# A 768-token windowed attention with a routed expert layer: second weights ordered behind row gathers, and one copy moved from ScalarE to VectorE

## The chip, the cores and the metric

The kernel runs on one core of one Trainium2 chip. The metric is the device time of one execution in microseconds; less is better. The engines are called as in the profile: PE (matrix products), PEld (its weight loads), DVE (VectorE), ACT (ScalarE), POOL (GpSimd) and SP (which issues most transfers here). An engine works through its own instructions in order, and waits on semaphores for the others and for transfers.

## The reference

Everything is float32. An attention with a local window and a few global keys makes x; each row of x then goes to one of eight experts, chosen by the largest cosine logit, and the expert's two products are scaled by the gate.

```python
batch, n_heads, seq, head_dim = (4, 8, 768, 64)
...
a = np.exp(scores)
a = a / (np.sum(a, axis=-1, keepdims=True) + 1e-09)
return np.matmul(a, v).astype(np.float32)
...
logits = xn @ en.T / tau
expert_idx = np.argmax(logits, axis=1)
...
for e in range(E):
    mask = expert_idx == e
    h = np.maximum(x[mask] @ w1[e], 0.0)
    out[mask] = gate_w[mask, None] * (h @ w2[e])
```

x has 3072 rows of 512; w1 of an expert is 512 x 1024 and w2 is 1024 x 512, 2 MB each.

## The kernel before, in words

The first 184 us compute the attention and the routing, and write x and a list of rows per expert to HBM. The first 256 rows of expert 0 are handled at the end of that part. Then a loop over the eight experts begins (L1880 on); an expert's rows that remain are padded to one of several widths.

In the loop, expert e is multiplied while the rows and weights of the next one ("coming") are fetched:

- **Rows.** POOL gathers rows of x by index. For experts 0 and 1 it gathers whole rows of 2 KB, 128 at a time (`gather_tiles`, L1056). From expert 2 on it gathers quarters: 16 gathers per expert, each of 128 quarter rows of 512 bytes (`gather_quarters`, L1082). While expert e runs, POOL issues the last eight quarters of expert e+1, then the scatters of results that are pending, then the first eight quarters of expert e+2, and then a drain. For expert 2 the first four come ahead and the other twelve in one go. Every two gathers after the first four, a tiny POOL copy (`landed`, L1081) waits until an earlier pair has landed; it holds the pace.
- **Weights.** SP loads w1 in four transfers of 512 KB (L169) and w2 in one of 2 MB (L170), both in `load_weights`. Two sets of buffers are used in turn. The first w1 transfer waits for a product of the expert before (`n.out_again`; for expert 2, for a scatter). The w2 transfer has no wait but that its buffer is free, which is when the expert two places earlier has done its last product. For experts 0 and 1 the weights come in 32 pieces of 128 KB each (`load_weights_part`, L182): 16 of w1, then 16 of w2. Those that the attention part has not issued are left in `n.weights` (L909): here three pieces of w1 and sixteen of w2, all of expert 1. The first of these waits for expert 0's first two row gathers.
- **Products.** The width of an expert selects an arm of a switch (`tc.Switch`, L1508), which the engines that take part enter by a branch: PE and ACT for expert 0, and DVE too from expert 1 on. In an arm PE makes the first product (L1414 for expert 0; from expert 1 on seven products in place of eight, L1437, with sums made by DVE and ACT at L1447, L1449, L1461 and L1466), then parts of the second (L1355, L1371). Behind the arm PE makes the other part from sums of weights and of hidden values (L1205), again seven for eight. DVE makes the sums of w2, `wsum`, at L1142 to L1145, the sums of w1, `fsum`, at L1167 to L1170, and turns gathered quarters by L1091.
- **Copies of turned tiles.** For experts 0 and 1 PE turns the gathered rows (L1114 in `turn_row`), and an engine copies the turned tile from PSUM (L1117). Ahead of the loop expert 0's tile 0 is copied by DVE and tile 1 by ACT; DVE then goes on with casts of the row lists, 16 small `squares`, `split_rows`, and the first zeros of the result tiles (`y_arm`, L1878).

ACT's last work ahead of an arm is part of a result tile `y` (L1256), which has to wait until the scatter that last read the buffer has landed. The order on every engine in this stretch is the order in which the program is written. The PSUM tiles `big`, which hold PE's products, are four.

Of the kernel before, what the change touches and what calls it, by code (L numbers as in the profile page):

```python
# [20 lines left out]
P = 128  # L21
NEG = 1e9
CAP = 512
PIECES = 32
# [138 lines left out]
    yield  # L163


def load_weights(k, e, w):
    nc = k.nc
    src = k.w1[e].rearrange("(p c) f -> c p f", p=P)
    first = [nc.sync.dma_start(w[0][:, c, :], src[c]) for c in range(k.NC)][0]  # L169
    nc.sync.dma_start(w[1][:], k.w2[e].rearrange("(f p) m -> p f m", p=P))  # L170
    return first


def load_weights_part(k, e, w, i):

    n = PIECES // 2
    src, dst, i = (k.w1[e], w[0], i) if i < n else (k.w2[e], w[1], i - n)
    rows, cols = dst.shape[1], dst.shape[2]
    per = n // rows
    r, c = i // per, cols // per * (i % per)  # L180
    src = src.rearrange("(r p) c -> p r c", p=P)
    return k.nc.sync.dma_start(dst[:, r, c : c + cols // per], src[:, r, c : c + cols // per])  # L182
# [891 lines left out]
def gather_quarters(k, ids, xgs, lo, hi):  # L1074

    src = k.x_dram[:, :].rearrange("t (b c) -> (t b) c", b=4)
    for i in range(lo, hi):
        j, g = divmod(i, 4)
        if g % 2 == 0 and i - lo > 3:
            m, h = divmod(i - 4, 4)  # L1080
            k.nc.gpsimd.tensor_copy(out=k.landed[0:1, 0:2], in_=xgs[m][0:1, h * P : (h + 2) * P : P])  # L1081
        k.nc.gpsimd.indirect_dma_start(  # L1082
            out=xgs[j][:, g * P : (g + 1) * P], out_offset=None, in_=src,
            in_offset=bass.IndirectOffsetOnAxis(ap=ids[:, j, g : g + 1], axis=0),
        )


def turn_squares(k, xgs, xT, j):
# [94 lines left out]
def hidden_sums(k, a):  # L1183
    return left_sums(k, a, k.hsum)
# [552 lines left out]
def kernel(  # L1737
# [13 lines left out]
    n = Net()  # L1751
    n.tc, n.nc = tc, tc.nc
    nc = n.nc
# [24 lines left out]
    with ExitStack() as moe:  # L1778
        wp_a = moe.enter_context(tc.tile_pool(name="wp_a", bufs=1))
        n.w = [new_weights(n, wp_a)]  # L1780
        def second_weights():
            n.wp_b = moe.enter_context(tc.tile_pool(name="wp_b", bufs=1, side="right", reuse_waits="tile"))
            return n.wp_b

        n.second_weights = second_weights
        n.ea = moe.enter_context(tc.tile_pool(name="ea", bufs=1))
        n.ea2 = moe.enter_context(tc.tile_pool(name="ea2", bufs=FIRST // P))
        with tc.manual_schedule(engines=ORDERED), ExitStack() as inner:
            window_attention(n, inner)

        n.big = ctx.enter_context(tc.tile_pool(name="big", bufs=4, space=PSUM, reuse_waits="tile"))
        n.work = ctx.enter_context(tc.tile_pool(name="work", bufs=3, space=PSUM, reuse_waits="tile"))
        n.work0 = ctx.enter_context(tc.tile_pool(name="work0", bufs=1, space=PSUM, reuse_waits="tile"))
        expert_pools(n, moe)
        n.tp = moe.enter_context(tc.tile_pool(name="sums", bufs=1, reuse_waits="tile"))
        n.late = moe.enter_context(tc.tile_pool(name="late", bufs=2, reuse_waits="tile"))

        arm_p = moe.enter_context(tc.tile_pool(name="arm_y", bufs=1))
        ys = []
        for i in range(2):  # L1800
            parts = {s: arm_p.tile([P, n.DM * s // P], F32, name="y%d_%d" % (s, i)) for s in (64, 32)}
            ys.append((arm_p.tile([P, CAP // P - 1, n.DM], F32, name="y_arm%d" % i), parts))

        n.wsum = n.tp.tile([P, 4, 4, 256], F32, name="wsum")
        n.hsum = n.tp.tile([P, 4, 4, P], F32, name="hsum")
        n.fsum = n.tp.tile([P, 3, 2, n.F // 2], F32, name="fsum")
        n.xsum = n.tp.tile([P, 3, 2, CAP // 2], F32, name="xsum")
        n.mt = n.const.tile([P, n.E, CAP // P, 3], F32, name="mts")
        n.ids = n.const.tile([P, n.E, CAP // P, 2], I32, name="idss")

        def numbers(lo, hi):
            for e in range(lo, hi):
                at = e * n.SL
                if e == 0:
                    at = nc.values_load(n.si[0:1, 0:1], engines=(SP,), min_val=0, max_val=FIRST)
                i = nc.sync.dma_start(n.mt[:, e], n.meta[bass.ds(at, CAP), :].rearrange("(j p) w -> p j w", p=P))
                wait_for(n, i, n.scatters)

        def cast(lo, hi, engine=nc.vector):
            engine.tensor_copy(out=n.ids[:, lo:hi], in_=n.mt[:, lo:hi, :, 0:2])  # L1820

        opened = {}

        def rows_of(e):
            if e not in opened:
                opened[e] = [n.xgp.tile([P, n.DM], F32, name="xg", tag="xg") for _ in range(CAP // P)]
            return opened[e]

        def prepare(e):
            t = Net()  # L1830
            t.e = e
            t.y, t.y_part = ys[e % 2]
            if e < 2:
                xgs, t.gathers = gather_rows(n, n.ids[:, e], n.xgp, now=None if e else 2)
            else:
                xgs = rows_of(e)
                gather_quarters(n, n.squares[:, e], xgs, *((0, 4) if e == 2 else (8, 16)))
            t.rows = n.mt[:, e], n.ids[:, e], xgs
            if e < 2:
                t.w = n.w[e]  # L1840
            else:
                t.w = new_weights(n, (wp_a, n.wp_b)[e % 2])
            return t

        with tc.manual_schedule(engines=ORDERED | set(ARMS) | {mybir.EngineType.Pool}):
            choose_widths(n)
            sums, making = weight_sums(n, n.w[0][1])
            wait_for(n, making[0](), [n.issued])
            for make in making[1:]:
                make()  # L1850
            numbers(0, 2)
            a = [[h[:, :, i * P : (i + 1) * P] for h in n.first.hT] for i in range(2)]
            left, making = hidden_sums(n, a)
            making[0]()
            cast(0, 1, nc.gpsimd)
            coming = prepare(0)
            gathers = coming.gathers
            for make in making[1:]:
                make()
            cast(1, 2)  # L1860
            numbers(2, n.E)
            for e, i in n.weights:
                part = load_weights_part(n, e, n.w[e], i)
                wait_for(n, part, gathers)
                gathers = []
            widths = [take_width(n, 0), take_width(n, 1)]
            give_hint(n, 0, widths[0])
            pair = Pair(n, n.first.rows, a, left, n.w[0][1], sums)
            pair.begin(True)
            unfinished = [pair.end_apart]  # L1870
            coming.xT = new_turned(n)
            for j in range(2):
                turn_row(n, coming.rows, coming.xT, j, (nc.vector.tensor_copy, nc.scalar.copy)[j])
            cast(2, n.E)
            square_rows(n)
            split_rows(n, n.mt)
            for x in (ys[0][0], *ys[0][1].values()):
                nc.vector.memset(x[:], 0.0)  # L1878
            first, making = first_sums(n, n.w[1][0])
            for make in making:  # L1880
                make()
            pending = []
            for e in range(n.E):
                now, coming = coming, None
                parts_of(n, now)
                now.width = widths[e]
                if e == 1:
                    now.first_sums = first
                if e + 1 < n.E:
                    coming = prepare(e + 1)  # L1890
                if e == 0:
                    gather_tiles(n, n.ids[:, 0], now.rows[2], range(2, CAP // P))
                for scatter in pending:
                    scatter()
                if e == 1:
                    gather_quarters(n, n.squares[:, 2], coming.rows[2], 4, 16)
                if 0 < e < n.E - 2:
                    gather_quarters(n, n.squares[:, e + 2], rows_of(e + 2), 0, 8)
                if e and coming:
                    wait_for(n, load_weights(n, e + 1, coming.w), [n.outs[-1] if e == 1 else n.out_again])  # L1900

                nc.gpsimd.drain()
                pending = expert(n, now, coming, widths, unfinished)
            for scatter in pending + unfinished.pop()():
                scatter()
# [31 lines left out]
```

## Time and profile before

| | us |
|---|---|
| median of three timed runs | 499.12 |
| lowest and highest of them | 495.23, 499.17 |
| the profiled execution, its own time | 501.52 |
| its span, first to last instruction | 499.8 |
| PE busy in that span | 480.6 (96%) |
| DVE, ACT, POOL busy | 327.5, 183.9, 222.4 |

All times in rows are microseconds from the start of the span, unless ns is written. In a row of the timeline the first number is the start, the second the stretch from start to end, then engine, line, operation, what it writes and reads, and how many instructions were merged; in square brackets stands how long the engine had been idle and what ended the idle time, where the profile names something. "<-issue" means that it names nothing. Names of transfers that SP issued stand at their issue, and a DMA that ended an idle time is inferred from semaphores.

### The profile page before, as it was taken

What the parts mean: (1) busy time and instruction counts of PE and PEld (TensorE: products, weight loads), DVE (VectorE), ACT (ScalarE), POOL (GpSimd) and SP (SyncE); (2) the same over time, 40 slices, a digit from 0 to 9 for tenths busy, and PEclk for the clock granted to TensorE, in tenths of its full rate; (3) what the DMA queues carried; (4) which work ended last, traced back from release to release, by engine and by line L of the source; (5) the groups of instructions that cost most, each with busy time, mean ns of one, the idle gap of its engine ahead of it and who ended that gap; (6) DMA issues with size and microseconds to landing.
All of it is one profiled execution on the core that took longest, in us unless ns stands there. A gap on an engine that the chain in (4) does not pass through costs nothing.

```text
span 499.8 us, 13595 instructions
## 1 busy us (share of the span) xinstructions
PE 480.6 (96%) x5474; PEld 398.0 (80%) x5474; DVE 327.5 (66%) x659; ACT 183.9 (37%) x448; POOL 222.4 (45%) x259
## 2 busy tenths in 40 slices
PE   7999999998999998999999999999999999999995
PEld 7677787786777887779788579889789689869964
DVE  5655887785798775657668646877855765736531
ACT  3856676675675411302212121422312321221220
POOL 4211102211333644476547745764874754833013
PEclk9999999999999999999999999999998999999998
DMA  8998999979574738429651256274382184111001
GB/s 164 194 190 190 209 229 210 230 169 205 165 201 136 181 31 244 147 78 359 203 200 37 71 198 206 83 254 161 105 294 81 46 259 178 53 66 60 0 23 70
DMA packets 116344, 77.20 MB, mean 154 GB/s; under 512 B 91998, under 2 KB 100190, under 8 KB 116202
## 3 DMA queue, kind: packets, MB, share of 16 engines
q1 hardware_dynamic: 106537, 59.86, 46.3%
q0 software_dynamic: 8064, 15.27, 9.8%
q8 instruction: 63, 1.03, 0.9%
q14 instruction: 80, 0.65, 0.4%
q10 hardware_dynamic: 1600, 0.39, 0.4%
HBM read 62.52 MB, written 17.16 MB: 159 GB/s over the span
## 4 chain that ended last, share of the span: by engine, by line
PE 76%; issue 8%; DMA 4%; POOL 4%; ACT 3%; DVE 3%; POOLq 0%; ACTq 0%; DVEq 0%
PE big L1437 22%; PE big L1205 9%; PE od L528 8%; PE work L1355 7%; PE pa L499 6%; PE od L538 4%; PE pa L476 4%; PE pa L704 3%; PE work L1205 3%; DMA xg<-x_dram,squares 2%; PE work L1371 2%; POOL out_dram L1390 2%; PE pa L601 2%; POOL xg L1082 2%; ACT ex L505 1%
## 5 line engine op out<-in xcount | busy, mean ns | idle before, releaser
L1082 POOL DMA_INDIRECT xg<-x_dram,squares x96 | 102.9, 1072 | 64.8 <-issue 45.5
L512 DVE TENSOR_TENSOR ex<-ex,table 126x768 f32<-126x768 f32 x64 | 59.8, 944 | 34.4 <-ACT ex L505 34.4
L1447 DVE TENSOR_TENSOR hT<-big,hT 128x320 f32<-128x320 f32 (+4 forms) x70 | 39.0, 563 | 44.2 <-PE big L1437 35.5
L505 ACT ACTIVATE ex<-pa 126x384 f32<-126x384 f32 (+1 forms) x128 | 54.0, 480 | 30.4 <-PE pa L499 29.5
L1437 PE MATMUL big<-xT,w1t 128*128 128x160 f32 (+4 forms) x336 | 60.7, 335 | 1.9 <-ACT hT L1461 1.9
L1437 PEld LDWEIGHTS big<-xT,w1t 128*128 128x128 f32 x336 | 55.9, 193 | 4.8 <-ACT hT L1461 2.2
L271 POOL DMA_INDIRECT meta<-mt,slot x24 | 25.5, 1065 | 57.9 <-PE pa L499 30.4
L528 PE MATMUL od<-ex,v 126*64 126x192 f32 (+1 forms) x576 | 46.0, 305 | 0.0
L1449 ACT ACTIVATE hT<-hT 128x320 f32<-128x320 f32 (+4 forms) x42 | 22.3, 531 | 57.1 <-DVE hT L1447 57.1
L499 PE MATMUL pa<-qT,kT 64*32 64x128 f32 (+3 forms) x2048 | 39.2, 265 | 3.1 <-issue 2.6
L499 PEld LDWEIGHTS pa<-qT,kT 64*32 64x32 f32 (+1 forms) x2048 | 30.2, 106 | 14.3 <-issue 9.4
L528 PEld LDWEIGHTS od<-ex,v 126*64 126x64 f32 x576 | 34.6, 136 | 7.7 <-issue 3.7
L1437 PE MATMUL big<-xsum,fsum 128*128 128x160 f32 (+4 forms) x224 | 40.1, 333 | 0.0
L1437 PEld LDWEIGHTS big<-xsum,fsum 128*128 128x128 f32 x224 | 36.9, 193 | 1.7 <-DVE fsum L1169 0.4
L1390 POOL DMA_INDIRECT out_dram<-y_arm,tids x17 | 18.0, 1057 | 40.5 <-ACT ptmp L1231 34.2
L1355 PE MATMUL work<-w2t,hT 128*128 128x512 f32 x80 | 35.1, 593 | 0.0
L1205 PE MATMUL big<-wsum,hsum 128*128 128x256 f32 x136 | 30.9, 380 | 0.1
L1205 PEld LDWEIGHTS big<-wsum,hsum 128*128 128x128 f32 x136 | 25.8, 190 | 4.4 <-issue 0.9
L1355 PEld LDWEIGHTS work<-w2t,hT 128*128 128x128 f32 x80 | 15.1, 190 | 17.7 <-issue 17.6
L1205 PE MATMUL big<-w2t,hT 128*128 128x256 f32 x112 | 26.7, 382 | 0.9 <-PE work L1371 0.9
L1205 PEld LDWEIGHTS big<-w2t,hT 128*128 128x128 f32 x112 | 21.0, 190 | 6.5 <-issue 4.0
L1091 DVE STREAM_TRANSPOSE xT<-xg 128x512 f32<-128x512 f32 x24 | 25.6, 1090 | 0.8 <-DMA xg<-x_dram,squares 0.8
(254 smaller groups left out, 854.7 us busy)
## 6 DMA issues: line engine op xcount, KB each, us to landing
w1t<-in_moe_w_dram SPq DMA_DIRECT2D x24, 512.0 KB
w2t<-in_moe_w_dram SPq DMA_DIRECT2D x6, 2048.0 KB
v<-in_v_dram SPq DMA_DIRECT2D x32, 192.0 KB
x_dram<-xs SPq DMA_DIRECT2D x23, 256.0 KB
k<-in_k_dram SPq DMA_DIRECT2D x28, 192.0 KB
q<-in_q_dram SPq DMA_DIRECT2D x28, 192.0 KB
w1t<-in_moe_w_dram SPq DMA_DIRECT2D x32, 128.0 KB
w2t<-in_moe_w_dram SPq DMA_DIRECT2D x32, 128.0 KB
```

The lines of the kernel that those rows point to most:

```text
L271: i = nc.gpsimd.indirect_dma_start(out=k.meta[:], out_offset=bass.IndirectOffsetOnAxis(ap=slot[:, t : t + 1], axis=0), in_=mt[:, t, :], in ...
L499: i = nc.tensor.matmul(u.sp[e][k0:k1, a * n + c0 : a * n + c1], lhsT=t.kT[rows, key + k0 : key + k1], rhs=t.qT[rows, j * BLK + c0 : j * BL ...
L505: nc.scalar.activation(u.ex[:, e], u.sp[e][0:ROWS, 0 : 2 * u.n].rearrange("p (a c) -> p a c", a=2), AF.Exp, scale=k.scale)
L512: nc.vector.tensor_tensor(out=exv, in0=exv, in1=tab[:, :, 0 : u.n // BLK, :], op=ALU.mult)
L528: nc.tensor.matmul(g.od[a][e * D : (e + 1) * D, at : at + c1 - c0], lhsT=g.v[0:ROWS, 2 * a + e, u.j, :], rhs=u.ex[:, e, a, c0:c1], start=f ...
L1082: k.nc.gpsimd.indirect_dma_start(out=xgs[j][:, g * P : (g + 1) * P], out_offset=None, in_=src, in_offset=bass.IndirectOffsetOnAxis(ap=ids[ ...
L1091: k.nc.vector.transpose(out=xT[:, :, :, j * half : (j + 1) * half].rearrange("p c a (g i) -> p g c a i", i=LACE), in_=xgs[j][:].rearrange( ...
L1205: i = self.k.nc.tensor.matmul(ps, lhsT=x[:, f, :], rhs=w[:, f, :], start=f == 0 and not add, stop=True, skip_group_check=True)
L1355: k.nc.tensor.matmul(ps, lhsT=self.hT[:, f, j * P : (j + 1) * P], rhs=self.w2[:, f, :], start=i == 0, stop=i == k.NF - 1, skip_group_check ...
L1390: i = k.nc.gpsimd.indirect_dma_start(out=k.out.rearrange("t (i m) -> (t i) m", i=n), out_offset=bass.IndirectOffsetOnAxis(ap=ids, axis=0), ...
L1437: nc.tensor.matmul(to[f // 2][:, f % 2 * 256 : f % 2 * 256 + h], lhsT=x[:, l, f * P : (f + 1) * P], rhs=y[:, l, 0:h], start=not (add or f ...
L1447: nc.vector.tensor_tensor(out=to, in0=x, in1=z, op=ALU.add)
```

## The change

Three edits:

1. `load_weights` returns its first w1 transfer and its w2 transfer. `gather_quarters` returns what it issues. In the loop, for experts 2 to 7, the w2 transfer also waits for the gather number `SOON` = 5, the sixth, of the quarters that were last issued for that same expert: the sixth of twelve for expert 2, the sixth of the last eight for the others.
2. Both of expert 0's turned tiles are copied by DVE, where ACT copied the second.
3. Of the nineteen pieces of expert 1's weights, the three of w1 stay where they are, and the sixteen of w2 are issued inside the loop, once expert 1's four row gathers have landed.

```diff
+SOON = 5
...
-    nc.sync.dma_start(w[1][:], k.w2[e].rearrange("(f p) m -> p f m", p=P))
-    return first
+    return first, nc.sync.dma_start(w[1][:], k.w2[e].rearrange("(f p) m -> p f m", p=P))
...
-            for e, i in n.weights:
-                part = load_weights_part(n, e, n.w[e], i)
-                wait_for(n, part, gathers)
-                gathers = []
+            def load_rest(parts, behind):
+                for e, i in parts:
+                    wait_for(n, load_weights_part(n, e, n.w[e], i), behind)
+                    behind = []
+
+            rest = [x for x in n.weights if x[1] >= PIECES // 2]
+            load_rest([x for x in n.weights if x not in rest], gathers)
...
-                turn_row(n, coming.rows, coming.xT, j, (nc.vector.tensor_copy, nc.scalar.copy)[j])
+                turn_row(n, coming.rows, coming.xT, j, nc.vector.tensor_copy)
...
                 if e == 0:
+                    load_rest(rest, coming.gathers)
+                if e == 0:
                     gather_tiles(n, n.ids[:, 0], now.rows[2], range(2, CAP // P))
...
-                    gather_quarters(n, n.squares[:, 2], coming.rows[2], 4, 16)
+                    coming.quarters = gather_quarters(n, n.squares[:, 2], coming.rows[2], 4, 16)
...
-                    wait_for(n, load_weights(n, e + 1, coming.w), [n.outs[-1] if e == 1 else n.out_again])
+                    first, second = load_weights(n, e + 1, coming.w)
+                    wait_for(n, first, [n.outs[-1] if e == 1 else n.out_again])
+                    wait_for(n, second, [coming.quarters[SOON]])
```

On ACT, at the end of the work ahead of the loop, this stood before, from the last work on a result tile through the entry of expert 0's arm to the first two copies of hidden values in it:

```order
L1256 ACTIVATE y<-big,emt 128x256
L1246 ACTIVATE ptmp<-ptmp,emt 128x256
L1117 COPY xT<-work 128x4x64 x2
L1932 SWITCH_STRIDE
L1932 ISA x2
L1508 BRANCH_PREFETCH_HINT
L1416 ACTIVATE hT<-big 128x2x4x16 x6
```

and this stands there now (L1416 has become L1420):

```order
L1260 ACTIVATE y<-big,emt 128x256
L1250 ACTIVATE ptmp<-ptmp,emt 128x256
L1943 SWITCH_STRIDE
L1943 ISA x2
L1512 BRANCH_PREFETCH_HINT
L1420 ACTIVATE hT<-big 128x2x4x16 x6
```

The two copies of a turned tile are gone from ACT, whose next instruction is now the entry of the arm. On DVE, at the same place, four copies stand where two did, ahead of the cast of the row lists, the `squares` and `split_rows`. Before:

```order
L1210 TENSOR_TENSOR ptmp<-big,ptmp 128x256 x2
L1217 SCALAR_TENSOR_TENSOR y<-big,emt,ptmp 128x256
L1117 COPY xT<-work 128x4x64 x2
L1820 CAST idss<-mts 128x48
L1070 TENSOR_SCALAR squares<-mts 32x24 x16
```

Now:

```order
L1214 TENSOR_TENSOR ptmp<-big,ptmp 128x256 x2
L1221 SCALAR_TENSOR_TENSOR y<-big,emt,ptmp 128x256
L1121 COPY xT<-work 128x4x64 x4
L1824 CAST idss<-mts 128x48
L1072 TENSOR_SCALAR squares<-mts 32x24 x16
```

On SP no transfer changes its place; only waits are added. DMASW names semaphores of POOL's transfers, DMAHW those of SP's. The last pieces of w1 of expert 1 and the first of w2, before:

```order
L182 DMA w1t<-in_moe_w_dram 128x256 [waits DMAHW1_49,DMASW5_49,DMASW4_49]
L182 DMA w1t<-in_moe_w_dram 128x256 [waits DMAHW2_49]
L182 DMA w1t<-in_moe_w_dram 128x256 [waits DMAHW3_49]
L182 DMA w2t<-in_moe_w_dram 128x256 [waits DMAHW4_49]
L182 DMA w2t<-in_moe_w_dram 128x256 [waits DMAHW5_49]
```

and now:

```order
L184 DMA w1t<-in_moe_w_dram 128x256 [waits DMAHW1_49,DMASW5_49,DMASW4_49]
L184 DMA w1t<-in_moe_w_dram 128x256 [waits DMAHW2_49]
L184 DMA w1t<-in_moe_w_dram 128x256 [waits DMAHW3_49]
L184 DMA w2t<-in_moe_w_dram 128x256 [waits DMASW7_49,DMASW6_49,DMAHW4_49,DMASW1_49,DMASW0_49]
L184 DMA w2t<-in_moe_w_dram 128x256 [waits DMAHW5_49]
```

The first piece of w2 now waits for four of POOL's gathers; the others stand behind it in SP's order. The whole w2 of a later expert stands between two groups of w1 transfers. Before:

```order
L170 DMA w2t<-in_moe_w_dram 128x8x512 [waits DMAHW2_49,DVE_49,PE_49]
L169 DMA w1t<-in_moe_w_dram 128x1024 [waits DMAHW3_49,DMAHW4_49,DVE_49,PE_49]
L169 DMA w1t<-in_moe_w_dram 128x1024
L169 DMA w1t<-in_moe_w_dram 128x1024 [waits DMAHW5_49]
L169 DMA w1t<-in_moe_w_dram 128x1024 [waits DMAHW6_49]
```

and now:

```order
L173 DMA w2t<-in_moe_w_dram 128x8x512 [waits DMASW6_49,DMAHW2_49,DVE_49,PE_49]
L172 DMA w1t<-in_moe_w_dram 128x1024 [waits DMAHW3_49,DMAHW4_49,DVE_49,PE_49]
L172 DMA w1t<-in_moe_w_dram 128x1024
L172 DMA w1t<-in_moe_w_dram 128x1024 [waits DMAHW5_49]
L172 DMA w1t<-in_moe_w_dram 128x1024 [waits DMAHW6_49]
```

The w2 transfer waits for one gather more, and the next expert's w1 stands behind it on SP.

## Rows read from the trace of the kernel before

**Rows 1.** The page: busy time of each engine, and the shares of the chain that ended last.

```profile
PE 480.6 (96%) x5474; PEld 398.0 (80%) x5474; DVE 327.5 (66%) x659; ACT 183.9 (37%) x448; POOL 222.4 (45%) x259
...
PE 76%; issue 8%; DMA 4%; POOL 4%; ACT 3%; DVE 3%; POOLq 0%; ACTq 0%; DVEq 0%
```

**Rows 2.** The waits of PE from 184 us to 500 us, the three longest: who waited for whom, total us, times, longest.

```profile
PE big L1437 <- ACT hT L1461: 1.9, 1, 1.9
PE big L1414 <- ACT hT L1416: 1.9, 1, 1.9
PE big L1205 <- PE work L1371: 0.9, 1, 0.9
```

**Rows 3.** The timeline at the entry of expert 0's arm: ACT, then PE, then DVE.

```profile
191.59 0.50 ACT L1246 ACTIVATE ptmp<-ptmp,emt 128x256 f32<-128x256 f32 x1
193.81 0.65 ACT L1117 COPY xT<-work 128x256 f32<-128x256 f32 x2 [1.73 <-PE work L1114]
200.66 0.89 ACT L1416 ACTIVATE hT<-big 128x160 f32<-128x160 f32 x4 [6.21 <-DMA w2t<-in_moe_w_dram]
...
194.56 4.58 PE L1414 MATMUL big<-xT,w1t 128*128 128x160 f32 x32 [0.78 <-ACT xT L1117]
201.02 2.44 PE L1414 MATMUL big<-xT,w1t 128*128 128x160 f32 x16 [1.88 <-ACT hT L1416]
...
193.43 0.74 DVE L1117 COPY xT<-work 128x256 f32<-128x256 f32 x2
```

**Rows 4.** The timeline at the entry of expert 5's arm (two rows of ACT, one of PE) and of ACT at the entry of expert 4's (last two).

```profile
368.93 0.47 ACT L1256 ACTIVATE y<-big,mts 128x256 f32<-128x256 f32 x1 [3.42 <-DMA out_dram<-y,idss]
375.06 0.86 ACT L1461 COPY hT<-big 128x384 f32<-128x384 f32 x2 [5.66 <-issue]
...
375.60 4.13 PE L1437 MATMUL big<-xT,w1t 128*128 128x192 f32 x16 [1.94 <-ACT hT L1461]
...
332.11 0.47 ACT L1256 ACTIVATE y<-big,mts 128x256 f32<-128x256 f32 x1 [0.18 <-PE big L1205]
335.26 0.45 ACT L1461 COPY hT<-big 128x352 f32<-128x352 f32 x1 [2.68 <-PE big L1437]
```

**Rows 5.** Stretches: length, busy time of PE, PEld, DVE, ACT and POOL with instructions, then the granted clock of PE (1.00 is 2.4 GHz, 0.50 is 1.2 GHz), the busy share of the DMA engines, and GB/s.

```profile
377.00:380.40 3.40, 3.40 (x13) 3.40 (x12) 1.00 (x1) 0.98 (x2) 2.08 (x3) 0.50 0.09 25
...
369.00:378.00 9.00, 7.06 (x41) 6.76 (x40) 4.48 (x5) 1.76 (x4) 5.21 (x7) 0.95 0.78 272
378.00:385.00 7.00, 7.00 (x37) 7.00 (x36) 2.72 (x4) 0.52 (x2) 3.11 (x4) 0.83 0.10 26
```

**Rows 6.** The timeline of SP: its weight transfers for experts 1, 2, 5 and 6.

```profile
191.15 1.29 SPq L182 DMA_DIRECT2D w1t<-in_moe_w_dram  x3
192.48 11.57 SPq L182 DMA_DIRECT2D w2t<-in_moe_w_dram  x16
222.65 1.77 SPq L169 DMA_DIRECT2D w1t<-in_moe_w_dram  x4
224.53 0.55 SPq L170 DMA_DIRECT2D w2t<-in_moe_w_dram  x1
...
334.01 0.39 SPq L170 DMA_DIRECT2D w2t<-in_moe_w_dram  x1
358.13 2.03 SPq L169 DMA_DIRECT2D w1t<-in_moe_w_dram  x4
368.49 0.38 SPq L170 DMA_DIRECT2D w2t<-in_moe_w_dram  x1
```

**Rows 7.** The timeline of POOL: expert 0's two row gathers and the last of expert 1's four; then for expert 5 the first and the sixth of the last eight quarters and two of the pacing copies; then the scatter that frees ACT's result tile.

```profile
186.60 0.97 POOL L1056 DMA_INDIRECT xg<-x_dram,idss  x1 [0.30 <-issue]
191.64 0.95 POOL L1056 DMA_INDIRECT xg<-x_dram,idss  x1 [0.30 <-issue]
...
344.98 1.05 POOL L1082 DMA_INDIRECT xg<-x_dram,squares  x1 [6.54 <-issue]
350.80 0.18 POOL L1081 COPY landed<-xg 1x2 f32<-1x2 f32 x1
352.41 1.41 POOL L1082 DMA_INDIRECT xg<-x_dram,squares  x1 [0.31 <-DMA xg<-x_dram,squares]
353.81 0.55 POOL L1081 COPY landed<-xg 1x2 f32<-1x2 f32 x1
362.76 1.15 POOL L1390 DMA_INDIRECT out_dram<-y,idss  x1 [0.30 <-issue]
```

**Rows 8.** The timeline of POOL for expert 6: two pacing copies with a w2 in flight, and the restart after its first eight quarters.

```profile
371.74 0.36 POOL L1081 COPY landed<-xg 1x2 f32<-1x2 f32 x1
376.99 0.17 POOL L1081 COPY landed<-xg 1x2 f32<-1x2 f32 x1 [2.51 <-DMA xg<-x_dram,squares]
383.17 0.94 POOL L1082 DMA_INDIRECT xg<-x_dram,squares  x1 [3.28 <-issue]
```

**Rows 9.** The timeline of DVE: the first reads of w2 of expert 1 and of expert 5.

```profile
225.01 1.22 DVE L1142 TENSOR_TENSOR wsum<-w2t 128x1024 f32<-128x1024 f32 x1
369.71 1.23 DVE L1142 TENSOR_TENSOR wsum<-w2t 128x1024 f32<-128x1024 f32 x1 [1.78 <-issue]
```

**Rows 10.** The timeline of ACT behind the arms of experts 3 and 4: its first instruction after the arm.

```profile
321.60 0.73 ACT L1378 ACTIVATE y<-work,pgate 128x256 f32<-128x256 f32 x2 [2.66 <-PE work L1371]
356.22 0.73 ACT L1378 ACTIVATE y<-work,pgate 128x256 f32<-128x256 f32 x2 [4.44 <-PE work L1371]
```

More of the change, by code (lines that the diff above doesn't have):

```diff
@@ L1076, in gather_quarters @@
     src = k.x_dram[:, :].rearrange("t (b c) -> (t b) c", b=4)
+    issued = []
     for i in range(lo, hi):
@@ L1081, in gather_quarters @@
             k.nc.gpsimd.tensor_copy(out=k.landed[0:1, 0:2], in_=xgs[m][0:1, h * P : (h + 2) * P : P])
-        k.nc.gpsimd.indirect_dma_start(
+        issued.append(k.nc.gpsimd.indirect_dma_start(
             out=xgs[j][:, g * P : (g + 1) * P], out_offset=None, in_=src,
             in_offset=bass.IndirectOffsetOnAxis(ap=ids[:, j, g : g + 1], axis=0),
-        )
+        ).ins)
+    return issued
 def turn_squares(k, xgs, xT, j):
@@ L1836, in prepare @@
                 xgs = rows_of(e)
-                gather_quarters(n, n.squares[:, e], xgs, *((0, 4) if e == 2 else (8, 16)))
+                t.quarters = gather_quarters(n, n.squares[:, e], xgs, *((0, 4) if e == 2 else (8, 16)))
             t.rows = n.mt[:, e], n.ids[:, e], xgs
```

## The prediction

> **What bounds the kernel now.** I read the page first: PE is busy 480.6 of 499.8 us and the chain that ended last lies 76% on PE [rows 1]. So an edit that moves copies and transfers can only win where PE stands still, or where its clock is low. The change touches nothing ahead of 184 us. I then asked for PE's waits behind that point: the longest two, 1.9 us each, are waits for ACT's first instruction in an arm, and the next is 0.9 [rows 2].
>
> The timeline shows the two places. At expert 0 ACT ends its copy of a turned tile at 194.46 and begins the arm's first copy of hidden values only at 200.66, 6.2 us later. PE has filled its four PSUM tiles by 199.14 and waits 1.88 us [rows 3]. The row names a w2 piece as the releaser; that is inferred, and the copy does not read w2. At expert 5 ACT ends its last work ahead of the arm at 369.40 and begins in it at 375.06, with 5.66 us for which nothing is named. At expert 4 the same step took at most 2.68 us, and there it was PE that ACT waited for [rows 4]. What differs: at expert 0 the sixteen w2 pieces are being issued from 192.48 on, and at expert 5 a w2 of 2 MB was issued at 368.49, half a microsecond ahead of ACT's last instruction, while at expert 4 the w2 went out at 334.01, 1.4 us behind it [rows 4, 6]. So entering an arm takes ACT up to 2.7 us, and about 6 us with weights in flight.
>
> A second price hangs on expert 5: behind PE's wait the granted clock is 0.50 from 377.0 to 380.4, that is 1.2 GHz [rows 5]. Half of 3.4 us is 1.7 us. With PE's wait of 1.94 [rows 4] expert 5's entry costs 3.65 us. Expert 0's wait was not followed by a low clock in this execution.
>
> Why is ACT late at expert 5? It stood idle from 365.51 on, for 3.42 us, and what ended that was the landing of a scatter out of the result tile that it was to fill [rows 4]; POOL had issued that scatter only at 362.76 [rows 7]. POOL was late because it stood still for 6.54 us before the last eight quarters of expert 5 [rows 7], with the w2 issued at 334.01 in flight: 2 MB move in 8 to 9 us (272 GB/s from 369 to 378, 26 behind that [rows 5]). Without weights in flight the same standstill is 3.28 us [rows 8].
>
> **The change, part by part.**
>
> *The copy on DVE.* DVE's two copies of tile 0 end at 194.17; two more of the same form take another 0.74, to 194.91. ACT's ended at 194.46 and PE began 0.10 later [rows 3], so PE begins at about 195.0, 0.45 us late. The bounds are 0 (copies fully overlapped with something else) and 0.74; I take 0.45. The casts, the sixteen `squares` and the zeros behind it on DVE move by 0.74 too; POOL's next quarter gathers wait for them, but these rows belong to expert 2, which PE multiplies only behind all of expert 1. ACT, in exchange, is free at 192.09 (the row of L1246) instead of 194.46. Even if its entry again takes 6.2 us it is in the arm at 198.3, ahead of 199.6, when PE's four tiles are full. So the wait of 1.88 goes, whatever the pieces do. Gain 1.88 - 0.45 = 1.43.
>
> *The sixteen pieces.* They wait for expert 1's four gathers. Expert 0's second gather ended its issue at 187.57, and SP went on at 191.15: 3.6 us to land [rows 6, 7]. Expert 1's last ends at 192.59, so the pieces start at about 196.2 instead of 192.48, and with 11.57 us of issue the last goes out at 207.8. DVE first reads that w2 at 225.01 [rows 9], 17 us later; SP's next transfer is at 222.65. Cost 0. What it may win, a faster entry of ACT, is already covered by the edit above.
>
> *The w2 behind the sixth gather.* SP waits up to the landing, and the only thing queued behind is the next w1. For expert 2 the w1 (222.65) and the w2 (224.53) were issued together [rows 6] and go through one queue, so w2 moved only behind w1 anyway; I take 0. The tightest is expert 5. The sixth of its gathers ends its issue at 353.82. Pairs landed within 3.0 us without weights in flight (POOL finished issuing a pair at 350.80, where its pacing copy begins, and the copy that waits for that pair ran at 353.81 [rows 7]), and 5.25 us lie between pacing copies with a w2 in flight [rows 8]. With POOL as it was, w2 would go out between 356.8 and 359.1, and land 9 us later, at 366 to 368, for a first read at 369.71 [rows 9]. But the w2 is no longer in flight when POOL stands still, so I take 3.28 for 6.54: POOL is 3.3 us earlier, w2 goes out at about 354 and lands at 363, ahead of the w1 of 358.13. Slack 6.7 us, cost 0.
> POOL's scatter moves with it, from 362.76 to 359.5. ACT went on 6.2 us behind it, at 368.93, so at 365.7 now, where ACT's work before it ended anyway at 365.51. ACT then does L1256 as soon as PE's product is there, within 1.3 us by my estimate, and enters with no w2 in flight, since expert 6's waits for its own sixth gather, and those eight began only at 383.17 [rows 8]. Entry by the 2.7 us of expert 4: 367.3 + 2.7 = 370.0; PE waited from 375.60 - 1.94 = 373.66 on, so ACT is there in time. The wait and the low clock go: gain 3.65.
>
> That whole step rests on weights in flight making others wait: 6.54 us against 3.28 for POOL's standstill, 5.7 to 6.2 against 2.7 for ACT's entry [rows 3, 4, 7, 8]. The Trainium skill, "DMA: Bandwidth & Descriptors", section "Queues, rings and completion order", speaks against it: a DMA engine goes round the queues that have work and changes after each packet. By that a gather or a small transfer waits for a packet of the weights and not for the rest of them, the place of w2 would be worth nothing, and the sum would be 1.43 in place of 5.08. I go by the rows, and the rule's result is the first rival.
>
> **Sum.** 1.43 + 3.65 = 5.08. From the profiled execution's own 501.52 (span 499.8 and 1.7 around it) that gives 496.4. The profiled execution is 2.4 above the median of the runs shown, 499.12. Two of those runs stand at 499.1 and 499.2 and one at 495.23: 3.9 lower, about the size of expert 5's term. I read this as runs with and without that wait. From the median: 499.12 - 5.08 = **494.0**; from the low run, which has only expert 0's term to lose: 493.8.
>
> **The rivals.**
>
> *Expert 5's wait stays, or was not in the median run.* The length of an entry may have nothing to do with weights: ACT's idle time is given to "issue", and only two long entries are there to judge by. Or POOL gains nothing, the w1 of 358.13 queues behind a w2 issued at 357, and is itself in flight when ACT enters. For it: one of three runs was low already. Against it: both long entries have weights in flight. Then only expert 0's term is won: 499.12 - 1.43 = 497.7. Chance 0.18. This is also what the rule quoted from the Trainium skill ("DMA: Bandwidth & Descriptors") would give.
>
> *The moved w2 meets ACT as it leaves an arm.* Leaving is a branch as well. Behind the arms of experts 3 and 4 ACT was idle 2.66 and 4.44 us, ended by PE [rows 10]. If leaving took 5.66 with a w2 now in flight there, ACT would be 3.0 and 1.2 us late, 4.2 in all if every bit reached PE: 494.0 + 4.2 = 498.2. For it: w2 of expert 5 from 354 to 363 covers 356. Against it: ACT leaves at 351.8, ahead of it. Chance 0.12.
>
> *Slower: the sixth gather becomes the clock of the weights.* Place: expert 5's w2. If its four pairs of gathers go at 5.25 us each instead of 3.0, because expert 5's w1 or the scatters are in the way, the sixth ends 9 us later, at 362.8, lands 5.25 later, at 368.1, and w2 lands at 377.1. DVE's first read at 369.71 is then 7.4 us late; the sums of PE's products stand behind it on DVE, so PE is late by as much: 499.12 - 1.43 + 7.4 = 505.1. It decides when w2 lands past 371.1, where expert 0's gain is used up: a sixth gather landing past 362. Against it: it has to lose 3 to 5 us on the pace of the trace, and two of the things that slowed POOL have moved away. Chance 0.06.
>
> **How the numbers follow.** About 1% (5 us) is what a measurement of this kernel tells from no change; the bounds are 494.1 and 504.1. The forecast has 0.64, and its time lies right at the lower bound: I put 0.36 below it and 0.28 above, since an earlier POOL may shorten other small waits. Same gets 0.28 + 0.18 + 0.12 = 0.58, slower 0.06. The likeliest case alone runs from 492.4 (from the low run, with no delay from the copy, 0.45, and PE's third wait, 0.9, gone too: 493.8 - 1.35) to 495.4 (the low clock gone only in part, 1.4 of its 1.7 us left). The range reaches up to the rivals at 497.7 and 498.2, to 498.5.
>
> **What would show it.** ACT's first instruction in expert 0's arm ahead of 199 us and no wait of PE for it; PE's first product there about 0.45 us later. In expert 5's arm ACT waits for PE and not the other way, and the granted clock shows 1.00 throughout. SP's w2 rows stand later than now, each behind its gather. POOL's standstills shrink towards 3.3 us. DVE's reads of w2 wait for nothing. Wrong it would be if a long entry of ACT shows up without weights in flight, or if DVE's first read of a w2 is ended by a transfer.

## The result and the profile after

The changed kernel takes **499.78 us** (median of 12 runs, 496.10 to 503.25), the kernel before, beside it, 497.31 (median of 12, 495.21 to 501.08; in the three runs shown with the forecast it was 499.12). The ratio is 1.0062, 95% interval 1.0032 to 1.0091: the change costs 1.6 to 4.5 us, where 5.08 were forecast to be won. The time lies above the range. The profiled execution spans 501.3 us, that of before 499.8. Six of the kernels below were measured while the kernel before, too, took 527 to 554 us; times from there are not used, and the executions of all others are called undisturbed.

What PE waits for from 190 us to 480 us, against [rows 2] (who waited for whom, total us, times, longest):

```profile
PE big L1209 <- issue: 2.3, 1, 2.3
PE big L1209 <- ACT y_arm L1365: 2.1, 1, 2.1
PE big L1418 <- DVE xT L1121: 1.2, 1, 1.2
PE big L1209 <- PE work L1128: 0.5, 1, 0.5
```

Both waits for ACT at an entry are gone. In their place stand two as long, on the products of L1209, the first that PE does behind an arm (L1205 before). The entries of experts 0 and 5 went as forecast; timeline, against [rows 3, 4]:

```profile
194.06 1.41 DVE L1121 COPY xT<-work 128x256 f32<-128x256 f32 x4
195.62 6.62 PE L1418 MATMUL big<-xT,w1t 128*128 128x160 f32 x47 [1.20 <-DVE xT L1121]
197.10 0.30 ACT L1420 ACTIVATE hT<-big 128x160 f32<-128x160 f32 x1 [4.38 <-PE big L1418]
...
369.02 2.76 PE L1441 MATMUL big<-xT,w1t 128*128 128x192 f32 x16
370.73 0.48 ACT L1465 COPY hT<-big 128x384 f32<-128x384 f32 x1 [2.76 <-PE big L1441]
```

At expert 0 the four copies on DVE end at 195.47 and PE waits 1.20 instead of 0.78 for its first product, then not again; ACT waits for PE. At expert 5 ACT is in the arm after 2.76 us of idling for PE, instead of 5.66.

Now the way out of expert 1's arm: first the stretches, with the columns of [rows 5], then the timeline.

```profile
230.00:234.00 4.00, 4.00 (x32) 4.00 (x31) 2.66 (x5) 1.88 (x4) 3.04 (x4) 1.00 0.34 78
234.00:238.00 4.00, 4.00 (x37) 2.59 (x35) 3.81 (x7) 0.94 (x2) 2.65 (x3) 1.00 1.01 379
238.00:242.00 4.00, 1.73 (x11) 1.38 (x8) 2.09 (x4) 0.33 (x1) 2.11 (x3) 1.00 0.46 165
```

```profile
231.45 0.38 SPq L173 DMA_DIRECT2D w2t<-in_moe_w_dram  x1
234.56 3.67 PE L1375 MATMUL work<-w2t,hT 128*64 128x256 f32 x32
240.50 1.97 PE L1209 MATMUL big<-w2t,hT 128*128 128x256 f32 x8 [2.27 <-issue]
241.67 0.73 ACT L1382 ACTIVATE y<-work,pgate 128x256 f32<-128x256 f32 x2 [6.01 <-PE big L1209]
```

Expert 2's w2 goes out at 231.45 and moves at 379 GB/s just when the arm is left. PE's last product in the arm ends at 238.23, its next begins at 240.50, and ACT's first instruction behind the arm comes later still, at 241.67: PE does not wait for ACT. What it waits for is its own sequencer. The rows of the line on which all branches are recorded (duration in ns: shortest, median, longest; then the first and last start in us) give the branch of PE's sequencer out of this arm, and the row of L1662 its first step behind it:

```profile
L1943 PEldq COMPARE_BRANCH  x1: 3798/3798/3798, 235.9 to 235.9; - x1
```

```profile
L1662 PEldq BRANCH_PREFETCH_HINT  x1: 39/39/39, 240.3 to 240.3; - x1
```

In the kernel before the same branch took 2.4 us, and PE waited 0.9:

```profile
L1932 PEldq COMPARE_BRANCH  x1: 2436/2436/2436, 236.7 to 236.7; - x1
```

The Trainium skill, "Runtime: NRT & Kernel Launch", section "Instruction fetch mechanics", says that a taken branch whose target is not among the instructions already loaded has to fetch them by DMA before the engine goes on. The traces agree with that picture: packets of two instruction queues (q8 and q14) begin within these branches, and begin later where weights are in flight (shown for expert 5's arm below).

Expert 5's arm, the timeline of the changed kernel, its branch, and the stretch behind the wait:

```profile
387.22 7.03 PE L1359 MATMUL work<-w2t,hT 128*128 128x512 f32 x16
387.64 0.38 SPq L173 DMA_DIRECT2D w2t<-in_moe_w_dram  x1
394.91 1.27 ACT L1365 ACTIVATE y_arm<-work,mts 128x512 f32<-128x512 f32 x2
396.39 3.65 PE L1209 MATMUL big<-w2t,hT 128*128 128x256 f32 x8 [2.14 <-ACT y_arm L1365]
```

```profile
L1943 PEldq COMPARE_BRANCH  x1: 7001/7001/7001, 388.6 to 388.6; - x1
```

```profile
397.00:400.00 3.00, 3.00 (x9) 2.38 (x8) 2.45 (x3) 0.00 (x0) 2.39 (x3) 0.52 0.56 203
```

The row blames ACT's L1365, but the branch ends at 395.6 and the product begins 0.8 later, as it does behind expert 1's arm; in the kernel before PE did this product ahead of that work of ACT:

```profile
L1932 PEldq COMPARE_BRANCH  x1: 3933/3933/3933, 391.8 to 391.8; - x1
```

```profile
397.25 1.89 PE L1205 MATMUL big<-w2t,hT 128*128 128x256 f32 x8
398.07 1.27 ACT L1361 ACTIVATE y_arm<-work,mts 128x512 f32<-128x512 f32 x2
```

There the branch took 3.9 us, hidden behind 7.03 us of products already queued; 7.0 us are not. Behind the wait the clock is granted at half (0.52 from 397 to 400), as it was behind expert 5's entry before [rows 5].

The DMA queues in the first 2.1 us of this branch (queue, kind, packets, MB, share of the 16 engines), first of the changed kernel, with w2 in flight:

```profile
q1 hardware_dynamic: 208, 0.43, 56.7%
q0 software_dynamic: 19, 0.02, 2.4%
```

then of the kernel before:

```profile
q0 software_dynamic: 32, 0.07, 11.3%
q8 instruction: 1, 0.02, 2.9%
q14 instruction: 1, 0.01, 1.7%
```

No instruction packet begins in the first stretch. By the times that the trace gives packets, the first one begins 0.32 to 0.33 us behind the start of this branch in all four profiles of the kernel before, and 2.2, 1.1 and 2.9 us behind it in the three of the changed one; out of expert 1's arm it is 0.1 to 0.6 against 1.3 to 1.7. So the fetch begins later when weights are in flight. Which engine a packet is for, the trace does not say.

### The profile page after: what moved, and what is told of

Same layout as the page of the kernel before. It is cut to its first block, busy times and chain, and to the rows that moved or that the text cites. A ratio compares the mean times of both kernels' runs of the same rounds, so it can differ in the third digit from the quotient of the medians.

```text
span 501.3 us, 13603 instructions
## 1 busy us (share of the span) xinstructions
PE 480.4 (96%) x5474; PEld 397.9 (79%) x5474; DVE 327.8 (65%) x661; ACT 184.0 (37%) x446; POOL 228.4 (46%) x259
## 4 chain that ended last, share of the span: by engine, by line
PE 88%; issue 3%; DMA 2%; ACT 2%; POOL 2%; SPq 1%; DVE 1%; ACTq 0%; POOLq 0%; DVEq 0%
PE big L1441 26%; PE big L1209 13%; PE od L530 8%; PE work L1359 7%; PE pa L501 6%; PE work L1209 4%; PE pa L478 4%; PE od L540 4%; PE work L1375 4%; PE pa L706 3%; PE pa L603 2%; PE big L1418 2%; PE work L1128 1%; POOL out_dram L1394 1%; PE pa L580 1%
## 5 line engine op out<-in xcount | busy, mean ns | idle before, releaser
L1441 PE MATMUL big<-xT,w1t 128*128 128x160 f32 (+4 forms) x336 | 59.3, 330 | 0.0
L1453 ACT ACTIVATE hT<-hT 128x320 f32<-128x320 f32 (+4 forms) x42 | 22.3, 531 | 56.7 <-DVE hT L1451 56.7
L1209 PE MATMUL big<-w2t,hT 128*128 128x256 f32 x112 | 28.5, 400 | 4.4 <-issue 2.3
L1209 PE MATMUL big<-wsum,hsum 128*128 128x256 f32 x136 | 30.9, 380 | 0.5 <-PE work L1128 0.5
L1209 PEld LDWEIGHTS big<-w2t,hT 128*128 128x128 f32 x112 | 22.0, 199 | 10.8 <-issue 5.0
L1209 PEld LDWEIGHTS big<-wsum,hsum 128*128 128x128 f32 x136 | 25.9, 191 | 4.9 <-issue 1.3
L1214 DVE TENSOR_TENSOR ptmp<-big,ptmp 128x256 f32<-128x256 f32 x16 | 6.7, 417 | 29.3 <-PE big L1209 29.3
```

What stands on the lines that cost most here:

```text
L1209: i = self.k.nc.tensor.matmul(ps, lhsT=x[:, f, :], rhs=w[:, f, :], start=f == 0 and not add, stop=True, skip_group_check=True)
L1441: nc.tensor.matmul(to[f // 2][:, f % 2 * 256 : f % 2 * 256 + h], lhsT=x[:, l, f * P : (f + 1) * P], rhs=y[:, l, 0:h], start=not (add or f ...
L1453: nc.scalar.activation(to, to, AF.Relu)
```

## The experiments

Single executions of one kernel lie 5 to 12 us apart, so medians of twelve hardly tell 1 us from nothing; the place of a cost is read from the profiles. Part of this scatter arises ahead of anything that an edit touches: PE's first product of expert 0 begins anywhere from 193.7 to 198.6 in the undisturbed profiles. Times of different chips are compared only with the kernel before on the same chip.

**One part at a time.** The first part alone, as a diff against the changed kernel:

```diff
-            load_rest([x for x in n.weights if x not in rest], gathers)
+            load_rest(n.weights, gathers)
...
-                turn_row(n, coming.rows, coming.xT, j, nc.vector.tensor_copy)
+                turn_row(n, coming.rows, coming.xT, j, (nc.vector.tensor_copy, nc.scalar.copy)[j])
...
-                if e == 0:
-                    load_rest(rest, coming.gathers)
```

> The kernel before with the first part of the change alone: w2 behind the sixth quarter gather, copies and pieces as before. Theory (weights in flight when an arm is left make PE and ACT wait for their next instructions): PE waits 1.9 us at expert 0's entry as before, none at expert 5's entry, about 2.3 us behind expert 1's arm (0.9 before) and about 2.1 us behind expert 5's, with granted clock 0.50 behind one of them; about 500.5 us against a median near 497.3, at least 1 us slower than before. Rival (the copy on DVE or the moved pieces cost what was lost): no long wait behind an arm, and about 495.5 us.

Measured 502.60 against 500.40, ratio 1.0056 (1.0023 to 1.0089): as large as the whole loss. Its longest waits of PE, and the half clock behind the first of them:

```profile
PE big L1209 <- issue: 2.6, 1, 2.6
PE big L1209 <- ACT y L1382: 0.9, 1, 0.9
```

```profile
243.00:247.00 4.00, 3.40 (x9) 2.75 (x10) 0.75 (x1) 1.89 (x4) 2.87 (x3) 0.57 0.22 61
```

The theory's places are right, with 0.9 instead of 2.1 behind expert 5's arm. One miss: PE's 1.9 us at expert 0's entry, which should have stayed, is 0.2 here.

The other two parts together (against the changed kernel), and the second alone (against the kernel before):

```diff
-                    wait_for(n, second, [coming.quarters[SOON]])
```

```diff
-                turn_row(n, coming.rows, coming.xT, j, (nc.vector.tensor_copy, nc.scalar.copy)[j])
+                turn_row(n, coming.rows, coming.xT, j, nc.vector.tensor_copy)
```

> The second and third part alone: both copies on DVE and the pieces behind expert 1's gathers, w2 where it was before. Theory (the loss is w2's alone): expert 0's wait of 1.9 us is gone, waits behind the arms of experts 1 and 5 stay at about 0.9 and 0, expert 5's entry wait is there in some runs as before: about 496 us, 1.4 below the kernel before. Rival (the copies or pieces cost the loss): 499 us or more.

> The kernel before with the copies on DVE alone. Theory: ACT enters expert 0's arm early enough even with the pieces in flight, so this is as fast as copies and pieces together, within 0.5 us, about 496 us. Rival (the pieces in flight stretch ACT's entry until PE waits all the same): PE's wait at expert 0 is still over 1 us, and the time is that of before, 497.3 us.

Measured 500.83 and 499.95 against the same 500.40; ratios 1.0050 (1.0004 to 1.0097) and 0.9963 (0.9922 to 1.0004). By the medians that is 0.4 slower and 0.5 faster; neither has the forecast gain of 1.43. The interval of copies and pieces lies above 1 (0.2 to 4.9 us slower), so by these times alone a loss from them, as the rival had it, is not excluded. Their profile cannot decide it: it shows only the 1.2 ahead of expert 0's first product, 0.7 behind expert 1's arm and 0.4 behind expert 0's, but it is of the fastest execution, 496.36. Against the rival stand the two kernels below that keep copies and pieces and move w2 elsewhere: they take as long as the kernel before.

PE's waits with the copies alone:

```profile
PE big L1205 <- issue: 1.8, 1, 1.8
PE big L1414 <- DVE xT L1117: 1.2, 1, 1.2
PE big L1437 <- ACT hT L1461: 0.5, 1, 0.5
PE big L1205 <- PE work L1124: 0.5, 1, 0.5
```

The 1.8 stands behind expert 1's arm, with w2 where it was before. There is no wait for ACT at expert 0, but a new one of 0.5 behind expert 0's arm (L1124). It stands in all nine profiles of undisturbed executions with both copies on DVE, 0.4 to 1.3 us, and in none of the five with a copy on ACT. PE's branch there takes 3.2 to 4.0 us in the nine (3.3 here) and 2.4 to 2.9 in the five.

**w2 at another place.** First behind the last of the eight gathers for the expert after next:

```diff
-                    gather_quarters(n, n.squares[:, e + 2], rows_of(e + 2), 0, 8)
+                    ahead = gather_quarters(n, n.squares[:, e + 2], rows_of(e + 2), 0, 8)
-                    wait_for(n, second, [coming.quarters[SOON]])
+                    if 1 < e < n.E - 2:
+                        wait_for(n, second, [ahead[-1]])
```

> The changed kernel, but the w2 of experts 3 to 6 waits for the last of the eight quarter gathers that POOL issues ahead (those of the expert after next), which land a few us behind an arm's entry; the w2 of experts 2 and 7 goes out as before. So no w2 should be in flight when an arm is left, and none at an entry. Theory: no PE wait over 1 us behind 196 us, no granted clock under 1.00 ahead of the end, about 494 us. Rival (what matters is POOL's standstill with a w2 in flight, which comes back here as 5 to 6.5 us and makes scatters late): PE waits for ACT at an entry as in the kernel before, about 497 us.

Measured 507.33 against 500.40, ratio 1.0126 (1.0068 to 1.0183). I had the wrong gathers: these come a whole expert later, so w2 was late for its readers, and both theories miss. SP, DVE and PE at expert 5:

```profile
371.72 0.39 SPq L173 DMA_DIRECT2D w2t<-in_moe_w_dram  x1
380.99 1.23 DVE L1146 TENSOR_TENSOR wsum<-w2t 128x1024 f32<-128x1024 f32 x1 [9.02 <-DMA w2t<-in_moe_w_dram]
383.88 4.55 PE L1441 MATMUL big<-xsum,fsum 128*128 128x192 f32 x16 [3.26 <-DVE hT L1451]
```

This is the price of the slower rival's mechanism, a w2 that lands behind DVE's first read: 9.0 us of DVE, 3.3 of PE.

Then behind the last of these eight gathers of the very expert whose w2 waits, and in a second kernel (its diff against the first) expert 2's w2 between two arms as well:

```diff
-                    gather_quarters(n, n.squares[:, e + 2], rows_of(e + 2), 0, 8)
+                    ahead[e + 2] = gather_quarters(n, n.squares[:, e + 2], rows_of(e + 2), 0, 8)[-1]
-                    wait_for(n, second, [coming.quarters[SOON]])
+                    if e > 1:
+                        wait_for(n, second, [ahead[e + 1]])
```

```diff
-                    if e > 1:
-                        wait_for(n, second, [ahead[e + 1]])
+                    wait_for(n, second, [ahead[e + 1] if e > 1 else coming.quarters[9]])
```

> in_arm once more: the w2 of experts 3 to 7 behind the last of the first eight quarter gathers of that same expert. Theory: ACT's branches at entries and exits 2.3 to 3.4 us, PE waits 0.7 to 1.8 behind expert 1's arm (w1 and w2 of expert 2 are in flight up to about 237 there) and nowhere else over 1 us behind 200 us; faster than the kernel before by 1.5 to 3 us. Rival: POOL's standstills with a w2 in flight make PE wait at entries 4 or 5, time as before or more.

> in_arm_and_gap once more: expert 2's w2 also between the exit of expert 1's arm and the entry of expert 2's. Theory: no PE wait over 0.5 us behind expert 1's arm; ACT's entry to expert 2's arm 5 us or more with a PE wait of 0 to 1.5 there; 0 to 1 us faster than in_arm_2. Rival: the long entry costs more than the exit gave, 1 us slower than in_arm_2.

Measured 499.34 and 499.49, before 499.34; ratios 1.0014 (0.9978 to 1.0049) and 0.9994 (0.9963 to 1.0025). PE's waits of the two:

```profile
PE big L1209 <- issue: 1.2, 1, 1.2
...
PE big L1209 <- PE work L1128: 0.9, 1, 0.9
```

```profile
PE big L1209 <- issue: 1.3, 1, 1.3
PE big L1418 <- DVE xT L1121: 1.2, 1, 1.2
```

The second kernel's stretch and branch behind expert 1's arm:

```profile
234.00:238.00 4.00, 4.00 (x35) 2.56 (x35) 3.81 (x6) 0.94 (x2) 3.53 (x4) 1.00 0.16 38
```

```profile
L1943 PEldq COMPARE_BRANCH  x1: 934/934/934, 235.4 to 235.4; - x1
```

There the 1.3 is behind expert 0's arm; behind expert 1's, with 38 GB/s in flight instead of 379, the branch takes 0.9 us and PE does not wait. These are the waits that the theory had (in in_arm_2 too: 1.2 behind expert 1's arm, 0.9 behind expert 0's). But the times are those of before. By the waits of its profile (2.5 us against a mean of 3.95 before, below) the second kernel should have won 1.45, which its interval (1.8 faster to 1.2 slower) holds but does not show. Moving w2 clear of the exits takes the loss back (the second kernel's interval lies below the changed kernel's, 1.0032 to 1.0091; the first one's overlaps it); that it does more is not shown.

Only expert 6's w2 moved, behind the eighth gather instead of the sixth (`7 if coming.e == 6 else SOON`):

> late_one once more: the changed kernel with expert 6's w2 alone behind the eighth quarter gather. Theory: no PE wait over 1 us and no low clock behind expert 5's arm, ACT's branch there 2.3 to 3.0 us; PE's wait behind expert 1's arm stays at 2.3 us. Rival: PE's wait behind expert 5's arm stays at 2 us.

It missed its aim: POOL was earlier in this execution, and w2 went out at 385.86, again ahead of the branch. Branch and wait:

```profile
L1943 PEldq COMPARE_BRANCH  x1: 6440/6440/6440, 388.9 to 388.9; - x1
```

```profile
PE big L1209 <- ACT y_arm L1365: 1.5, 1, 1.5
```

**The same kernels again.** Are the waits there every time? First the changed kernel:

> The changed kernel once more, for another profile. Theory: PE's long waits stand behind expert 1's arm (over 2 us) and, where w2 goes out as the arm is left, behind expert 5's (1 to 2.6); none at an entry over 1.3. Rival: they fall where chance puts them.

> The changed kernel, a further profile. Theory: PE waits over 2 us behind expert 1's arm every time, and behind expert 5's only where w2 goes out within 3 us ahead of the branch (0 where it goes out over 5 us ahead). Rival: the wait behind expert 1's arm is under 1 us in some executions.

Behind expert 1's arm PE waits 2.7 and 2.4 us. Behind expert 5's it waits 0 in the first, where w2 went out at 381.79 and the branch took 3.6 us, and 1.4 in the second, with 384.60 and 6.3. That second one misses its theory's "only within 3 us": w2 went out 4.75 us ahead of the branch (389.35). The rows of the first:

```profile
381.79 0.38 SPq L173 DMA_DIRECT2D w2t<-in_moe_w_dram  x1
```

```profile
L1943 PEldq COMPARE_BRANCH  x1: 3612/3612/3612, 387.8 to 387.8; - x1
```

The half clock came behind expert 1's wait in after_4 (0.50 from 241 to 244), and not at all in after_third. Now the kernel before:

> The kernel before once more, for a second profile of it (the prediction had one). Theory (the profile that the prediction was read from showed two waits that most executions do not have): at least one of the two waits at an entry, 1.88 us at expert 0 and 1.94 at expert 5, is under 0.5 us, and PE waits 0.7 to 1.8 us behind expert 1's arm and nothing over 0.5 behind expert 5's. Rival (they are there every time, and the changed kernel loses what it gains elsewhere): both over 1.5 us.

before_3 and before_4 had the same two theories. The waits of PE in the three, without the 0.8 ahead of expert 0's first product that each has:

```profile
PE big L1205 <- issue: 1.4, 1, 1.4
PE big L1437 <- ACT hT L1461: 0.9, 1, 0.9
```

```profile
PE big L1205 <- issue: 1.1, 1, 1.1
PE big L1414 <- ACT hT L1416: 0.7, 1, 0.7
```

```profile
PE big L1414 <- ACT hT L1416: 1.5, 1, 1.5
PE big L1205 <- PE work L1371: 0.8, 1, 0.8
```

Each lacks at least one of the two waits on which the forecast rested, expert 0's L1416 and expert 5's L1461, and none has the half clock ahead of the end.

**Not settled.** Two more kernels were to tell whether the pieces alone free expert 0's entry, and whether a kernel with all these waits removed is faster:

> The kernel before with expert 1's sixteen pieces of w2 behind its gathers and nothing else: one copy stays on ACT, w2 as before. Theory (pieces in flight stretch ACT's entry to expert 0's arm, and only that): no wait of PE for ACT at expert 0's entry, no wait over 0.3 us behind expert 0's arm, 0.7 to 1.8 behind expert 1's; about 1 us below before. Rival (the copies on DVE alone had freed that entry, and the gap behind expert 0's arm comes from the pieces): PE waits 0.5 to 1.9 at expert 0's entry, or 0.4 to 1.3 behind its arm.

> in_arm_and_gap with one of expert 0's copies back on ACT: pieces behind expert 1's gathers, no w2 in flight where an arm is left, and none at an entry but expert 2's. Theory (each wait has its own cause, and the DVE copies have a price of their own, 0.42 us ahead of PE's first product and 0.4 to 1.3 us behind expert 0's arm): behind 190 us PE waits 0.8 ahead of expert 0's arm and nowhere else over 0.7; 2 to 3 us below the kernel before. Rival (the waits of PE that were seen go elsewhere in most executions): no difference that can be measured, within 1 us of before.

The first is copies and pieces together with one copy back on ACT, the second in_arm_and_gap with one copy back on ACT. They, and the first runs of four kernels told above (in_arm, late_one, after_again, in_arm_and_gap), are the six whose times are not used; most of their waits, too, stand at places that no edit touches. Only the branches can be read. Out of expert 0's arm PE's took 2.9 us in pieces_only and 2.6 in w2_clear_copy_split, but 2.7 to 3.0 in the four with both copies on DVE, so it tells nothing here. Out of expert 1's arm it took 1.1 us in w2_clear_copy_split and 1.0 in in_arm_and_gap, with w2 clear of that exit, 2.6 in pieces_only and in_arm, with w2 as before, and 4.0 and 3.9 in late_one and after_again, with w2 as changed: the order seen above. Neither question is answered.

## Why the prediction was wrong

Means over the undisturbed profiles, four of before and three of after, give the balance in PE's time; they were taken on several chips, and a mean of three or four such values is rough:

| us | before | after |
|---|---|---|
| ahead of expert 0's first product | 0.8 | 1.2 |
| expert 0's entry | 1.9, 0, 0.7, 1.5: mean 1.0 | 0 |
| behind expert 0's arm | 0 | 0.5, 0.9, 0.7: mean 0.7 |
| behind expert 1's arm | 0.9, 1.4, 1.1, 0.8: mean 1.05 | 2.3, 2.7, 2.4: mean 2.5 |
| expert 5's entry | 1.9, 0.9, 0, 0: mean 0.7 | 0 |
| behind expert 5's arm | 0 | 2.1, 0, 1.4: mean 1.2 |
| half clock (1.7 each) | in 1 of 4: 0.4 | in 2 of 3: 1.1 |
| sum | 3.95 | 6.7 |

The difference, 2.75, agrees with the measured 2.47 between the medians. 2.65 of it are the first part's (1.45 + 1.2 + 0.7 - 0.7), and gate_only, with 2.2 between the medians, has about that, though copies and pieces, with an interval above 1, leave it open that a part is theirs.

- *The copy on DVE.* Its price, 0.45, measured 0.4: right. Expert 0's wait did go, but the term was sized from the one profile: 1.88 there, 1.0 on average. And the term lacked the 0.7 us behind expert 0's arm. So a gain of 1.43 became 1.0 - 0.4 - 0.7: nothing. What in the copies stretches PE's branch there is open.
- *Expert 5's entry.* In the first profile the steps came as forecast or earlier: POOL's standstill shrank from 6.54 to 3.61, w2 went out at 348.54 (forecast about 354), ACT was in the arm at 370.73 (forecast 370.0), the wait went. In the other two it went although the standstill stayed at 6.71 and 6.58, against 4.28 to 4.88 in the three new profiles of before; POOL began these gathers 8 to 11 us earlier there, having stood still 3.1 to 3.2 us instead of 7.5 to 7.8 ahead of the last eight of expert 4. So the step on this standstill held in one profile of three, and that the wait went does not rest on it alone. And the term was 3.65 in the one profile and 0.7 + 0.4 on average. The prediction noted that one run in three was low already, and still took the whole term from the median.
- *The moved w2 at a cost of 0* is the step that failed. It was weighed against its readers and against ACT's entries alone. Nobody asked which exits it would meet: expert 1's and expert 5's. The second rival named the mechanism, but on ACT, and at expert 4's exit, where PE lost nothing; the engine that pays is PE, whose own branch grows from 2.4 to 3.8 us and from 3.9 to as much as 7.0. What is in flight is not all that sets it: out of expert 5's arm it took 1.2 us in one profile of before (before_3) and 0.7 with the copies alone. The rival got 0.12 and 498.2 us.
- *The pieces at a cost of 0*: nothing in the profiles of the changed kernel speaks against it.
- *The rule of the Trainium skill* weighed in the prediction ("DMA: Bandwidth & Descriptors", section "Queues, rings and completion order"), by which a DMA engine changes between its queues after each packet, was taken there to mean that the place of w2 is worth nothing. The branches show that it is worth something: 0.9 us with 38 GB/s in flight, 3.8 with 379. A packet of w2 takes about 0.09 us here, by an estimate from the row of q1 above (56.7% of 16 engines for 2.1 us, 208 packets), and the first instruction packet began 2.2 us behind its branch, not 0.1. Whether a packet of the rule is a packet of the profile, no run shows.

Shown: the first part alone loses about as much as the whole change, PE's branch out of an arm is longer when a w2 is in flight there, and instruction packets begin later in it. Not shown: that the copies and the pieces cost nothing, which engine those packets serve, and that the kernel with w2 clear of the exits beats the one before.

## What to carry to other kernels

Before a bulk load is moved, list every branch of every engine in the stretch that it will occupy, exits as well as entries, and compare the branch's time with the work that its engine has queued. Where a wait stands beside an engine's branch, look at the branch's own row before believing the releaser. And size a gain from several executions: a wait of 2 us that one profile shows may be there in one of four.

## What was not expected of the hardware

- PE's branch out of the same arm took 0.9 us with 38 GB/s in flight, 2.4 with a w2 that had all but landed, 3.8 with 379 GB/s, and 7.0 out of another arm with a w2 issued 1.0 us ahead of it.
- Of the waits of PE of 1.9 to 2.7 us behind 190 us, some are followed by about 3.4 us at half clock and some are not: 2.66 us behind expert 1's arm was not, 2.44 at the same place was.
